# Two expert layers and an attention layer on one core: every first-layer weight split at one place, the next layer's weight conversion under a branch at one of two

## The chip, the cores and the metric

The kernel runs on one core of one Trainium2 chip. The metric is device time in microseconds (us) of one execution. The profile comes from one execution, and its times count from the start of its span.

## The reference, cut to what matters

Attention over 4 batches produces 2176 tokens of 512 values each. A router then gives each token one of 8 experts, and the expert is two matrix products with a relu between them. A third layer (two products with a convolution and a gate between) follows. In short:

```
x = attention(...)                       # 4 x 544 tokens x 512
e = argmax(x @ w_gate), or the expert of the token before where a local gate holds it
h = relu(x[token] @ w1[e])               # 512 -> 1024
out[token] = p[e] * (h @ w2[e])          # 1024 -> 512
y = (h2 * sigmoid(conv3(h2))) @ w_out,  h2 = relu(out @ w_in)
```

All of it is fp32. A product is made of three products of a high and a low part (`wh`, `wl` of a weight, `xh`, `xl` of an input), so a weight has to be split before it is used: ScalarE (ACT) casts the high part, VectorE (DVE) subtracts to get the low part.

## The kernel before

**Slots.** The tokens are sorted by expert into slots of 128. Slots 0 and 1 (`NA` is 2) are worked on beside the end of attention; slots 2 to 20 each have one `step(s)`, and slot 21 has `last`. An expert has several slots in a row. Its first slot can be a *few* slot: at most 32 tokens, for which the kernel reads the unsplit weights directly with narrow matmuls (`few()` in `layer1` and `layer2`); other slots use the split weights (`full()`).

**What one step does.** `step(s)` writes, in this order: the load of one raw chunk of the third layer's weights (`raw_load`, on SyncE's queue, SP); `layer1(s)`; the load of the next expert's first weight (`fetch(s, 1)`); the gather of slot s+3's tokens (`gather`, GpSimd, POOL); the transposes and the split of slot s+1's tokens (`turn_x(s + 1)`); the last instruction of the conversion begun one step earlier (`self.conv.pop()()`, called the pop below); the split of the first weight for slot s+1, if that slot's expert is new (`resplit(s + 1, 1)`); six DVE instructions and one POOL addition that convert the chunk of the third layer's weights from 64-bit to fp32 (`convert`, `conv64`); `layer2(s - 1)` and the load of the next second weight (`fetch(s - 1, 2)`); `turn_h(s)`, which splits the hidden values (`gh`, `gl`); and the split of the second weight if slot s's expert is new (`resplit(s, 2)`). Chunks are converted in steps 3 to 18.

**Order.** No scheduler moves anything: each engine executes its own part of this text in order, and waits on semaphores for what it reads. What an engine has in front of an instruction is therefore what the text has in front of it. Branches on a register (`tc.If`) are taken by every engine that has instructions in them, and the others pass a join.

**Two places for the first split.** The table `esi` holds in its row 1, for each slot, 0 if its expert is that of the slot before, 1 if it is new, and 2 if it is new and the slot is a few slot. A slot with 1 has its first weight split in the step before it (the early place, `resplit(s + 1, 1)`). A slot with 2 doesn't need the split weight itself; its split stands after its own `layer1` (the late place, `resplit(s, 1, late=True)`):

```
with self.tc.If(v == 2 if late else v == 1 if n == 1 else v != 0):
```

**Names in the rows.** `ws` is a raw expert weight, `wh` and `wl` its parts; `xs`, `xh`, `xl` are slot tokens; `hp` and `yp` the sums of layer 1 and layer 2; `gh`, `gl` the hidden values; `fx` a raw chunk and `wf` its conversion.

Of the kernel before, what the change touches and what calls it, by code (L numbers as in the profile page):

```python
# [13 lines left out]
ALU = mybir.AluOpType  # L14
AX = mybir.AxisListType
# [543 lines left out]
NSLOT = 25  # L559
NA = 2  # L560
NB = NSLOT - NA
# [94 lines left out]
class Routing:  # L656
# [15 lines left out]
    def tl(self, shape, name, dt=F32, tag=None):  # L672
        return self.rp.tile(shape, dt, name=name, tag=tag or name)
# [170 lines left out]
    def phase_b(self, rp, pst):  # L844
        nc, c, tl = self.nc, self.c, self.tl
        v = nc.vector
        self.rp = rp
        yield from self.front(1, pst)
        n = NT
# [46 lines left out]
        def over_s(t):  # L896
# [18 lines left out]
        esi = self.esi  # L915
        ch = tl([1, NB], "r_ch")
# [2 lines left out]
        v.tensor_reduce(nx, s1, AX.X, ALU.min)  # L919
        v.tensor_copy(esi[:, 0, NA:], es[:, 1:])  # L920
        v.tensor_copy(esi[:, 1, NA:], ch)
        v.scalar_tensor_tensor(esi[:, 1, NA + 1:NSLOT - 4], self.fw[:, 1:NB - 4], 1.0, ch[:, 1:NB - 4],
                               ALU.add, ALU.mult)
        v.tensor_copy(esi[:, 2, NA - 1:NA], es[:, 1:2])
        v.tensor_copy(esi[:, 3, NA - 1:NA], ch[:, 0:1])
        yield
# [10 lines left out]
    def few(self, b0, first):  # L937
        v, c, tl = self.nc.vector, self.c, self.tl
        sh = [1, NB, E]
        sm = tl([1, E], "r_sm")  # L940
        v.scalar_tensor_tensor(sm, b0, -128.0, first[0:1], ALU.mult, ALU.add)
        v.tensor_scalar(sm, sm, P - TS - 0.5, 1024.0, ALU.is_lt, ALU.mult)
        v.tensor_tensor(sm, sm, b0, ALU.add)
        eq = tl(sh, "r_s2")
        v.tensor_tensor(eq, sm[:, None, :].to_broadcast(sh), c.sl[0:1, :, None].to_broadcast(sh), ALU.is_equal)
        self.fw = tl([1, NB], "r_fw")
        v.tensor_reduce(self.fw, eq, AX.X, ALU.max)
        v.tensor_copy(self.esi[:, 5, NA:], self.fw)

    def late_tokens(self, s):  # L950
        v, tl = self.nc.vector, self.tl
# [72 lines left out]
class Weights:  # L1024
# [25 lines left out]
    def split(self, n, src, eng=None):  # L1050
        for k in range(len(self.t[n])):
            self.split_k(n, src, k, eng or (self.nc.gpsimd if k in POOL_K[n] else self.nc.vector))


class Moe:
# [156 lines left out]
    def last(self, s, cwr, cw):  # L1212
# [20 lines left out]
        self.fetch(s - 1, 2)  # L1233
        f2.load0()
        resplit(0, 4)
        for k in range(K_LAST, NKC - 1):
            self.l1_mm(xt, w, hp, k, range(2))
# [8 lines left out]
        for a in (0, 4):  # L1246
            self.lo_t(ht, a, t[a // 4])
        resplit(4, NFC)
        yp = self.y_tile()
        for k in range(NFC):  # L1250
# [37 lines left out]
        self.W.load(n, (self.w1, self.w2)[n - 1][bass.ds(e, 1)], **({"cond": c} if (s, n) != (0, 1) else {}))  # L1288

    def changed(self, s, pool=False):  # L1290
        return self.nc.values_load(self.rt.esi[0:1, 1, s:s + 1], min_val=0, max_val=2,
                                   engines=[mybir.EngineType.Activation, mybir.EngineType.Pool]
                                   + ([] if pool else [mybir.EngineType.DVE]))

    def resplit(self, s, n, eng=None, late=False):
        if (n == 1 and not late) or s < NA:
            self.chg[s] = self.changed(s, eng is not None)
        v = self.chg[s]
        with self.tc.If(v == 2 if late else v == 1 if n == 1 else v != 0):  # L1299
            self.W.split(n, self.W.s, eng)  # L1300

    def small(self, s):
# [4 lines left out]
    def either(self, s, few, all_):  # L1307
        with self.tc.If(self.sm[s] != 0) as c:
            few()
        with c.Else():  # L1310
            all_()

    def turn_x(self, s):
        nc = self.nc
        xs = self.xs[s]
        x = self.xt[s] = tuple(self.tp.tile([P, NKC, P], F32R, tag="x" + q, name="x" + q) for q in "hl")
        t = (self.ps if s == NA else self.px).tile([P, 4, P], F32, tag="tr", name="xlp")

        def turn():
            for k in range(NKC):  # L1320
                nc.tensor.transpose(t[:, k, :], xs[:, P * k:P * k + P], self.ident)

        def few():
            turn()
            raw()

        def raw():
            nc.scalar.copy(xs[:, 0:NKC * TS].rearrange("p (k t) -> p k t", t=TS), t[:, :, P - TS:P])

        def full():  # L1330
            turn()
            nc.scalar.copy(x[0], t)
            self.lo_t(x, 0, t)

        if s == NA:
            full()
            raw()
        else:
            self.either(s, few, full)

# [65 lines left out]
    def step(self, s):  # L1406
        W, hi = self.W, NSLOT - 3
        if NA < s <= NA + 16:
            self.raw_load(s - NA - 1)
        if s + 1 < hi - 1:  # L1410
            self.small(s + 1)
        self.layer1(s)
        if s > NA:
            self.resplit(s, 1, late=True)
        self.fetch(s, 1)
        if s + 3 < hi:
            self.xs[s + 3] = self.gather(s + 3)
        if s + 1 < hi - 1:
            self.turn_x(s + 1)
        else:  # L1420
            self.xt[s + 1] = self.hi_lo_t(self.xs.pop(s + 1), NKC, "x")
        while self.conv:
            self.conv.pop()()
        self.resplit(s + 1, 1)
        if NA < s <= NA + 16:
            self.convert(s - NA - 1)
        if s == NA:
            for _ in self.rest:
                pass
        else:  # L1430
            self.layer2(s - 1)
            self.fetch(s - 1, 2)
        self.turn_h(s)
        self.resplit(s, 2)

    def chunk(self, s):
        return (1, s // 2, 512 * (s % 2)) if s < 8 else (2, s - 8, 0)
# [422 lines left out]
```

## Time and profile before

| what | us |
|---|---|
| median of 3 runs | 645.39 (642.68 to 645.6) |
| the profiled execution, its own time | 643.43 |
| its span, first to last instruction | 641.7 |
| TensorE (PE) busy | 585.6 (91%) |
| DVE busy | 415.3 (65%) |
| ACT busy | 319.3 (50%) |
| POOL busy | 171.3 (27%) |

Attention's last products start at 149 us, slots 0 and 1 are done near 188 us, the steps run from 182 to 407 us, and the third layer's products start at 434.8 us. Which slots are new or few depends on the data; the timeline of ACT shows it, because a full slot's relu is line 1276, a few slot's is line 1352, and a weight split is line 1047 (4 casts of 1024 columns for a first weight, 8 of 512 for a second one). With the relu's start as the mark of a slot:

| slot | relu at, us | kind |
|---|---|---|
| 2 | 186.35 | few |
| 4 | 204.71 | new expert, full |
| 7 | 244.40 | new expert, full |
| 9 | 266.05 | new expert, few |
| 13 | 314.82 | new expert, few |
| 16 | 347.72 | new expert, few |
| 18 | 373.52 | new expert, full |
| 21 | 418.16 | new expert, full |

The other slots are full and go on with the expert of the slot before.

### The profile page before, as it was taken

What the parts mean: (1) busy time and instruction counts of PE and PEld (TensorE: products, weight loads), DVE (VectorE), ACT (ScalarE), POOL (GpSimd) and SP (SyncE); (2) the same over time, 40 slices, a digit from 0 to 9 for tenths busy, and PEclk for the clock granted to TensorE, in tenths of its full rate; (3) what the DMA queues carried; (4) which work ended last, traced back from release to release, by engine and by line L of the source; (5) the groups of instructions that cost most, each with busy time, mean ns of one, the idle gap of its engine ahead of it and who ended that gap; (6) DMA issues with size and microseconds to landing.
All of it is one profiled execution on the core that took longest, in us unless ns stands there. A gap on an engine that the chain in (4) does not pass through costs nothing. (4 is left out here: it accounts for less than half of the span.)

```text
span 641.7 us, 16204 instructions
## 1 busy us (share of the span) xinstructions
PE 585.6 (91%) x6066; PEld 483.6 (75%) x6066; DVE 415.3 (65%) x870; ACT 319.3 (50%) x634; POOL 171.3 (27%) x226
## 2 busy tenths in 40 slices
PE   7888888888988999979989899978899999999997
PEld 6666666766666888758767678758898998998986
DVE  7867577866956857785596984586983293393340
ACT  4754555564225454552454643665864374363331
POOL 7664910042032223223224230100032132300100
PEclk8999899999999999999999999998899999999999
DMA  8999658658047666575275673123101201000001
GB/s 223 217 218 235 186 126 189 194 194 287 18 158 272 218 210 227 185 264 197 84 261 182 247 281 125 51 89 86 50 1 51 81 3 49 34 1 34 33 35 50
DMA packets 60644, 90.57 MB, mean 141 GB/s; under 512 B 25726, under 2 KB 34198, under 8 KB 60504
## 3 DMA queue, kind: packets, MB, share of 16 engines
q1 hardware_dynamic: 57016, 78.93, 39.7%
q0 software_dynamic: 3520, 10.23, 4.7%
q8 instruction: 64, 1.05, 0.7%
q14 instruction: 44, 0.36, 0.2%
HBM read 125.87 MB, written 15.79 MB: 221 GB/s over the span
## 5 line engine op out<-in xcount | busy, mean ns | idle before, releaser
L1565 DVE SCALAR_TENSOR_TENSOR fc<-f_hp,cw,fc 128x544 f32<-128x544 f32 (+2 forms) x66 | 51.7, 784 | 72.8 <-ACT fc L1563 71.4
L1048 DVE TENSOR_TENSOR wl<-ws,wh 128x512 fp32r<-128x512 f32 (+1 forms) x92 | 74.4, 871 | 14.1 <-ACT wh L1047 12.5
L1047 ACT CAST wh<-ws 128x512 fp32r<-128x512 f32 (+1 forms) x96 | 66.2, 768 | 5.7 <-DMA ws<-in_moe_w_dram 5.3
L1128 PE MATMUL yp<-wl,gh 128*128 128x512 f32 x144 | 57.5, 399 | 3.6 <-DVEq L1299 3.3
L1128 PE MATMUL yp<-wh,gh 128*128 128x512 f32 x144 | 59.2, 411 | 1.1 <-ACTq L1299 0.9
L1128 PE MATMUL yp<-wh,gl 128*128 128x512 f32 x144 | 57.2, 397 | 0.0
L1112 PE MATMUL hp<-wl,xh 128*128 128x512 f32 x144 | 48.6, 409 | 7.7 <-DVEq L1299 7.1
L1623 PE MATMUL f<-wh,fh 128*128 128x512 f32 (+1 forms) x144 | 55.4, 385 | 0.0
L1623 PE MATMUL f<-wl,fh 128*128 128x512 f32 (+1 forms) x144 | 55.1, 383 | 0.0
L1623 PE MATMUL f<-wh,fl 128*128 128x512 f32 (+1 forms) x144 | 55.1, 382 | 0.0
L1112 PE MATMUL hp<-wh,xh 128*128 128x512 f32 x144 | 50.2, 421 | 2.8 <-ACT wh L1047 2.7
L278 ACT ACTIVATE pr<-sp,nm 128x128 f32<-128x128 f32 x128 | 36.5, 374 | 26.2 <-DVE nm L275 26.2
L1276 ACT ACTIVATE hs<-hp 128x512 f32<-128x512 f32 x36 | 19.9, 595 | 59.4 <-PE hp L1112 59.3
L1020 POOL TENSOR_TENSOR wf<-wf,fx 128x512 int32<-128x512 int32 x16 | 20.8, 1300 | 103.1 <-DVE fx L1019 75.3
L1112 PE MATMUL hp<-wh,xl 128*128 128x512 f32 x144 | 47.8, 404 | 0.0
L1073 POOL DMA_INDIRECT xs<-x_dram,gidx x22 | 26.3, 1194 | 73.6 <-ACT pr L278 34.1
L1085 POOL DMA_INDIRECT y_dram<-ys,sidx x22 | 23.6, 1070 | 70.9 <-ACT ys L1401 31.9
L1112 PEld LDWEIGHTS hp<-wl,xh 128*128 128x128 f32 x144 | 27.4, 194 | 16.8 <-DVEq L1299 9.3
L1570 ACT ACTIVATE f_hp<-f 128x544 f32<-128x544 f32 x31 | 19.4, 624 | 35.9 <-PE f L1546 35.7
L1128 PEld LDWEIGHTS yp<-wl,gh 128*128 128x128 f32 x144 | 27.2, 189 | 10.4 <-DVEq L1299 4.2
L1105 DVE TENSOR_TENSOR gl<-hlp,gh 128x512 fp32r<-128x512 f32 x36 | 23.3, 686 | 18.0 <-ACT gh L1378 16.3
L1632 ACT COPY fy<-f 128x512 f32<-128x512 f32 (+1 forms) x18 | 10.1, 563 | 48.6 <-PE f L1623 48.6
(382 smaller groups left out, 1506.3 us busy)
## 6 DMA issues: line engine op xcount, KB each, us to landing
ws<-in_moe_w_dram SPq DMA_DIRECT2D x42, 2048.0 KB
fx<-y_dram SPq DMA_DIRECT2D x17, 256.0 KB
raw<-in_k_l_dram SPq DMA_DIRECT2D x16, 256.0 KB
x_dram<-x SPq DMA_DIRECT2D x16, 256.0 KB
fx<-in_moe_w_in_dram SPq DMA_DIRECT2D x8, 512.0 KB
fx<-in_moe_w_out_dram SPq DMA_DIRECT2D x8, 512.0 KB
out_dram<-fy SPq DMA_DIRECT2D x16, 256.0 KB
VA<-in_v_l_dram SPq DMA_DIRECT2D x20, 192.0 KB
```

Of the source, the lines that this page charges most:

```text
L278: nc.scalar.activation(pr[:, hp, :], sp[:, hp, :], AF.Exp, bias=nm[:, hp:hp + 1], scale=-1.0)
L1020: nc.gpsimd.tensor_tensor(a, a, lo, ALU.add)
L1047: (cp.tensor_copy if cp else self.nc.scalar.copy)(h, src[n][:, k, :])
L1048: eng.tensor_tensor(l, src[n][:, k, :], h.bitcast(F32), ALU.subtract)
L1073: self.nc.gpsimd.indirect_dma_start(out=xs, out_offset=None, in_=self.x_dram[0:n, :], in_offset=bass.IndirectOffsetOnAxis(ap=self.rt.gidx[ ...
L1085: self.nc.gpsimd.indirect_dma_start(out=self.y_dram[:, :], out_offset=bass.IndirectOffsetOnAxis(ap=self.rt.sidx[:, s:s + 1], axis=0), in_= ...
L1105: self.nc.vector.tensor_tensor(hl[1][:, a:a + 4], t, hl[0][:, a:a + 4].bitcast(F32), ALU.subtract)
L1112: self.nc.tensor.matmul(hp[c], a[:, k, :], b[:, 512 * c:512 * c + 512], start=k == 0 and m == 0, stop=k == NKC - 1 and m == 2)
L1128: self.nc.tensor.matmul(yp, a[:, k, :], b, start=k == 0 and m == 0, stop=k == NFC - 1 and m == 2)
L1276: self.nc.scalar.activation(hs[:, 512 * c:512 * c + 512], hp[c], AF.Relu)
L1565: nc.vector.scalar_tensor_tensor(c[:, a:b], hp[:, a + t:b + t], self.cw[:, t, f:f + 1], c[:, a:b], ALU.mult, ALU.add)
L1623: self.nc.tensor.matmul(yp[:, cs], x[:, c], w[:, cs], start=f == 0 and n == 0, stop=f == NFC - 1 and n == 2)
```

## The change

Row 1 of `esi` holds only 0 or 1. The late place is gone, so a few slot's first weight is split in the step before it too. The conversion is written twice in each of steps 3 to 18, each time under a branch: at its old place if slot s+1 goes on with the same expert, and at the end of the step if slot s+1's expert is new. In the first of these steps (`turn_x` of slot 2), the copy for the few case stands ahead of the split.

```diff
@@ routing
         v.tensor_copy(esi[:, 1, NA:], ch)
-        v.scalar_tensor_tensor(esi[:, 1, NA + 1:NSLOT - 4], self.fw[:, 1:NB - 4], 1.0, ch[:, 1:NB - 4],
-                               ALU.add, ALU.mult)
...
-        self.fw = tl([1, NB], "r_fw")
-        v.tensor_reduce(self.fw, eq, AX.X, ALU.max)
-        v.tensor_copy(self.esi[:, 5, NA:], self.fw)
+        v.tensor_reduce(self.esi[:, 5, NA:], eq, AX.X, ALU.max)
@@ Moe
-    def resplit(self, s, n, eng=None, late=False):
-        if (n == 1 and not late) or s < NA:
+    def resplit(self, s, n, eng=None):
+        if n == 1 or s < NA:
             self.chg[s] = self.changed(s, eng is not None)
-        v = self.chg[s]
-        with self.tc.If(v == 2 if late else v == 1 if n == 1 else v != 0):
+        with self.tc.If(self.chg[s] != 0):
             self.W.split(n, self.W.s, eng)
...
+        def split():
+            nc.scalar.copy(x[0], t)
+            self.lo_t(x, 0, t)
+
         def full():
             turn()
-            nc.scalar.copy(x[0], t)
-            self.lo_t(x, 0, t)
+            split()
 
         if s == NA:
-            full()
+            turn()
             raw()
+            split()
@@ step
         self.layer1(s)
-        if s > NA:
-            self.resplit(s, 1, late=True)
         self.fetch(s, 1)
...
         self.resplit(s + 1, 1)
         if NA < s <= NA + 16:
-            self.convert(s - NA - 1)
+            with self.tc.If(self.chg[s + 1] == 0):
+                self.convert(s - NA - 1)
...
         self.turn_h(s)
         self.resplit(s, 2)
+        if NA < s <= NA + 16:
+            self.conv.pop()
+            with self.tc.If(self.chg[s + 1] != 0):
+                self.convert(s - NA - 1)
```

What follows are pieces of the program as each engine has it, without times. In the changed kernel the lines of the program have other numbers: 1048 becomes 1044, 1105 becomes 1101, 1014 to 1021 become 1010 to 1017, and the branches at 1299, 1303 and 1308 become 1294, 1298 and 1303.

On DVE before, between the early first split of a step (whose join is the first row) and the split of the hidden values, stand the six instructions of the conversion, whatever the next slot is:

```order
L1299 UNCONDITIONAL_BRANCH x2
L1014 TENSOR_SCALAR wf_3967<-fx 128x512
L1015 SCALAR_TENSOR_TENSOR wf_3967<-fx,wf_3967 128x512
L1016 TENSOR_SCALAR fx<-fx 128x512
L1017 TENSOR_SCALAR fx<-fx 128x512
L1018 SCALAR_TENSOR_TENSOR wf_3967<-fx,wf_3967 128x512
L1019 TENSOR_SCALAR fx<-fx 128x512
L1308 COMPARE_AND_BRANCH
L1308 UNCONDITIONAL_BRANCH x2
L1308 COMPARE_AND_BRANCH
L1308 UNCONDITIONAL_BRANCH
L1105 TENSOR_TENSOR gl<-hlp,gh 128x512 x2
```

They now stand under the branch of line 1423 there, and where it skips them the hidden split follows the weight split at once. DVE before, at the turn to the next step, after the second weight's split: the late first split stands between the step's first register load and the next slot's token split.

```order
L1303 TENSOR_LOAD esi
L1308 COMPARE_AND_BRANCH
L1308 UNCONDITIONAL_BRANCH x2
L1299 COMPARE_AND_BRANCH
L1048 TENSOR_TENSOR wl_0_2725<-ws_3446,wh_0_2724 128x1024
L1048 TENSOR_TENSOR wl_1_2727<-ws_3446,wh_1_2726 128x1024
L1048 TENSOR_TENSOR wl_2_2729<-ws_3446,wh_2_2728 128x1024
L1048 TENSOR_TENSOR wl_3_2731<-ws_3446,wh_3_2730 128x1024
L1299 UNCONDITIONAL_BRANCH x2
L1308 COMPARE_AND_BRANCH
L1308 UNCONDITIONAL_BRANCH
L1105 TENSOR_TENSOR xl<-xlp,xh 128x512
```

The same place on DVE in the changed kernel, where the first row is the branch around the second copy of the conversion:

```order
L1435 COMPARE_AND_BRANCH
L1010 TENSOR_SCALAR wf_3964<-fx 128x512
L1011 SCALAR_TENSOR_TENSOR wf_3964<-fx,wf_3964 128x512
L1012 TENSOR_SCALAR fx<-fx 128x512
L1013 TENSOR_SCALAR fx<-fx 128x512
L1014 SCALAR_TENSOR_TENSOR wf_3964<-fx,wf_3964 128x512
L1015 TENSOR_SCALAR fx<-fx 128x512
L1435 UNCONDITIONAL_BRANCH x2
L1298 TENSOR_LOAD esi
L1303 COMPARE_AND_BRANCH
L1303 UNCONDITIONAL_BRANCH x2
```

Four instructions under a branch have gone from ahead of the token split, and six under another branch have come. On POOL before, one step from its scatter to the conversion's addition reads as follows (the branch after the join of line 1308 is the late one):

```order
L1085 DMA y_dram<-ys_3453,sidx 2176x512
L1299 COMPARE_AND_BRANCH
L1299 UNCONDITIONAL_BRANCH x2
L1308 UNCONDITIONAL_BRANCH
L1299 COMPARE_AND_BRANCH
L1299 UNCONDITIONAL_BRANCH x2
L1308 UNCONDITIONAL_BRANCH
L1073 DMA xs<-x_dram,gidx 128x512
L1291 TENSOR_LOAD esi
L1299 COMPARE_AND_BRANCH
```

POOL in the changed kernel, the same piece:

```order
L1081 DMA y_dram<-ys_3453,sidx 2176x512
L1294 COMPARE_AND_BRANCH
L1294 UNCONDITIONAL_BRANCH x2
L1435 COMPARE_AND_BRANCH
L1016 TENSOR_TENSOR wf_3964<-wf_3964,fx 128x512
L1435 UNCONDITIONAL_BRANCH x2
L1303 UNCONDITIONAL_BRANCH x2
L1069 DMA xs<-x_dram,gidx 128x512
L1287 TENSOR_LOAD esi
L1294 COMPARE_AND_BRANCH
```

The second copy of the addition stands between a step's scatter and the next step's gather.

## Rows read from the trace of the kernel before

**Rows 1.** The page, busy time of an engine, share of the span, instructions.

```profile
PE 585.6 (91%) x6066; PEld 483.6 (75%) x6066; DVE 415.3 (65%) x870; ACT 319.3 (50%) x634; POOL 171.3 (27%) x226
```

**Rows 2.** Timeline of PE, steps 2 to 19: start, us, instruction [idle before, releaser].

```profile
184.25 1.93 PE L1350 MATMUL hp<-ws,xs 128*32 128x256 f32 x32 [1.75 <-ACT xs L1328]
...
199.42 0.74 PE L1112 MATMUL hp<-wl,xh 128*128 128x512 f32 x2 [0.53 <-DVE wl L1048]
...
207.29 0.50 PE L1128 MATMUL yp<-wl,gh 128*128 128x512 f32 x1 [1.78 <-DVEq L1299]
...
273.45 0.73 PE L1112 MATMUL hp<-wl,xh 128*128 128x512 f32 x2 [0.72 <-DVEq L1299]
...
286.31 0.74 PE L1112 MATMUL hp<-wl,xh 128*128 128x512 f32 x2 [3.31 <-DVEq L1299]
...
288.06 1.05 PE L1112 MATMUL hp<-wl,xh 128*128 128x512 f32 x2
...
333.31 0.73 PE L1112 MATMUL hp<-wl,xh 128*128 128x512 f32 x2 [1.63 <-DVEq L1299]
...
365.99 1.22 PE L1112 MATMUL hp<-wh,xh 128*128 128x512 f32 x2 [2.10 <-ACT wh L1047]
...
375.47 0.50 PE L1128 MATMUL yp<-wl,gh 128*128 128x512 f32 x1 [1.14 <-DVEq L1299]
```

**Rows 3.** Timeline of ACT, five places of steps 2 to 17.

```profile
182.54 0.59 ACT L1332 CAST xh<-xlp 128x512 fp32r<-128x512 f32 x1 [5.77 <-PE xlp L1321]
183.89 0.27 ACT L1328 COPY xs<-xlp 128x128 f32<-128x128 f32 x1 [0.76 <-DVE xl L1105]
...
197.06 3.89 ACT L1047 CAST wh<-ws 128x1024 fp32r<-128x1024 f32 x4 [0.98 <-DMA ws<-in_moe_w_dram]
...
307.08 0.27 ACT L1328 COPY xs<-xlp 128x128 f32<-128x128 f32 x1 [0.32 <-PE yp L1128]
...
364.90 3.89 ACT L1047 CAST wh<-ws 128x1024 fp32r<-128x1024 f32 x4 [2.48 <-DMA ws<-in_moe_w_dram]
```

**Rows 4.** Timeline of DVE, steps 3 and 4: a conversion and the two splits behind it.

```profile
202.69 0.42 DVE L1014 TENSOR_SCALAR wf<-fx 128x512 int32<-128x512 int32 x1
...
205.89 1.29 DVE L1105 TENSOR_TENSOR gl<-hlp,gh 128x512 fp32r<-128x512 f32 x2
208.40 0.69 DVE L1105 TENSOR_TENSOR xl<-xlp,xh 128x512 fp32r<-128x512 f32 x1 [1.22 <-DVEq L1299]
```

**Rows 5.** Timeline of DVE, steps 9 and 10.

```profile
275.28 0.43 DVE L1014 TENSOR_SCALAR wf<-fx 128x512 int32<-128x512 int32 x1 [1.94 <-DMA fx<-in_moe_w_in_dram]
...
278.94 5.63 DVE L1048 TENSOR_TENSOR wl<-ws,wh 128x512 fp32r<-128x512 f32 x8 [0.52 <-PE hp L1112]
284.90 0.69 DVE L1105 TENSOR_TENSOR xl<-xlp,xh 128x512 fp32r<-128x512 f32 x1 [0.34 <-DVEq L1299]
```

**Rows 6.** Timeline of SP: weight loads issued in steps 8 and 9.

```profile
258.14 5.39 SPq L1040 DMA_DIRECT2D ws<-in_moe_w_dram  x2
...
272.35 1.86 SPq L1040 DMA_DIRECT2D ws<-in_moe_w_dram  x2
```

**Rows 7.** Timeline of DVE, steps 12 and 13.

```profile
313.07 1.29 DVE L1105 TENSOR_TENSOR gl<-hlp,gh 128x512 fp32r<-128x512 f32 x2 [5.73 <-ACT gh L1378]
...
320.83 0.68 DVE L1105 TENSOR_TENSOR xl<-xlp,xh 128x512 fp32r<-128x512 f32 x1
321.43 0.68 DVE L1021 SCALAR_TENSOR_TENSOR wf<-wf,fx 128x512 int32<-128x512 int32 x1
322.26 0.43 DVE L1014 TENSOR_SCALAR wf<-fx 128x512 int32<-128x512 int32 x1
```

**Rows 8.** Timeline of DVE, step 17.

```profile
366.01 4.63 DVE L1048 TENSOR_TENSOR wl<-ws,wh 128x1024 fp32r<-128x1024 f32 x4
...
374.07 1.29 DVE L1105 TENSOR_TENSOR gl<-hlp,gh 128x512 fp32r<-128x512 f32 x2 [0.38 <-issue]
```

**Rows 9.** Timeline of POOL, the conversion's addition in step 13.

```profile
325.49 1.32 POOL L1020 TENSOR_TENSOR wf<-wf,fx 128x512 int32<-128x512 int32 x1 [9.50 <-DVEq L1308]
```

More of the change, by code (lines that the diff above doesn't have):

```diff
@@ L1290, in changed @@
     def changed(self, s, pool=False):
-        return self.nc.values_load(self.rt.esi[0:1, 1, s:s + 1], min_val=0, max_val=2,
+        return self.nc.values_load(self.rt.esi[0:1, 1, s:s + 1], min_val=0, max_val=1,
                                    engines=[mybir.EngineType.Activation, mybir.EngineType.Pool]
                                    + ([] if pool else [mybir.EngineType.DVE]))
-    def resplit(self, s, n, eng=None, late=False):
-        if (n == 1 and not late) or s < NA:
+    def resplit(self, s, n, eng=None):
+        if n == 1 or s < NA:
             self.chg[s] = self.changed(s, eng is not None)
-        v = self.chg[s]
-        with self.tc.If(v == 2 if late else v == 1 if n == 1 else v != 0):
+        with self.tc.If(self.chg[s] != 0):
             self.W.split(n, self.W.s, eng)
```

## The prediction

> **What bounds the kernel now.** I read the page first: TensorE is busy for 91% of the span [rows 1], so time can only come from the places where it waits. The timeline of TensorE alone, from 180 to 410 us, shows them. In a step between two full slots with one expert it has no gap. All gaps stand around slots 2, 4, 9, 13, 16 and 18, where an expert is new or a slot is few [rows 2]. Eight waits stand in the rows; the one at 273.45 has two more like it (for slots 14 and 17), and the one at 199.42 has one like it just before. Together that is about 15 us of waiting. After the longest wait the pairs of matmuls are slower too: a pair at 288.06 takes 1.05 us against the 0.73 of one right after a wait, which I estimate adds some 1.2 us over four such pairs; the first pair after the wait at 365.99 takes 1.22.
>
> The releasers are nearly all DVE. So I read DVE's timeline for what stood in front: a conversion that starts at 202.69 ahead of the hidden split `gl` at 205.89, which is 3.2 us, 3.1 of it the six instructions [rows 4]; the late first split and then a second split of 5.63 us behind a conversion that waits for its chunk's DMA [rows 5]. ACT's rows show two waits for a weight load [rows 3].
>
> **The change part by part.**
>
> *The conversion leaves the early place where slot s+1 is new* (steps 3, 6, 8, 12, 15, 17). In step 3, `gl` starts when the first split ends, some 3.1 us earlier; TensorE's wait of 1.78 at 207.29 [rows 2] is smaller than that, so all of it goes. In step 17, `gl` at 374.07 [rows 8] likewise comes 3.1 us earlier and the 1.14 at 375.47 goes. In step 6 nobody waits. The conversion then runs between `gl` and the next `xl`. For slot 5 that makes `xl` about 1 us later than 208.40, with TensorE still busy in layer 2 until about 211: hidden there. Terms: 1.8 and 1.1.
>
> *Slot 2's copy ahead of its split.* The copy starts at 182.54 in place of 183.89 [rows 3], so layer 1 of slot 2 starts and ends some 1.35 earlier. Slot 3's layer 1 then waits for its own `xl`, which stands behind gate work on DVE that hangs on slot 2's `xl`, now 0.3 later; I give nothing for that. But the load of slot 4's first weight is issued when layer 1 of slot 2 has read the buffer, and ACT waits 0.98 for this load at 197.06 [rows 3]. With the load 1.35 earlier that wait goes, and of TensorE's two waits, the 0.53 at 199.42 and its like, some 0.9 in all. Bounds 0 and 1.1; I take 0.9, since both waits hang on that one load.
>
> *Slots 13 and 16: the first split in the step before.* In step 12 ACT is free from the copy at 307.08 on [rows 3], so the cast starts near 307.6, and the DVE part 1.1 later (as 366.01 follows 364.90 [rows 3, 8]), to end 4.63 later at 313.3. `gl` of slot 12, at 313.07 before [rows 7], becomes 313.4 plus the price of skipping the early conversion (call it e). Then come 1.29 of `gl`, the skip of an eight-instruction second split, and the moved conversion. The skip's price is read from two rows: `xl` stands 1.22 behind `gl` where the second split was skipped [rows 4], and 0.34 behind a second split that ran [rows 5], so skipping eight instructions costs about 0.9. The conversion ends near 318.7 + e. The pop must now wait for POOL's addition (1.32 [rows 9]), so it starts near 320.1 + e, against 321.43 before [rows 7]. The chain from there (conversion, second split, next `xl`, TensorE at 333.31) is the same, with one more skip e before that `xl`. So it comes 1.3 - 2e earlier. e lies between 0.15 and 0.9: the skip of the four-instruction first split, which lies between the pop that ends at 322.11 and 322.26, takes 0.15 [rows 7]. Six instructions stand between four and eight; I take 0.3, nearer the four, because the moved block like the first split stands alone behind its branch, and book 0.7. Bounds 1.0 and -0.5. The wait of slot 14 that is like 273.45 also goes, but only moves TensorE up to the same later wait, so it isn't counted apart.
>
> For slot 16 the rows have the same form. Behind it slot 18's first weight waits for its load at 364.90 [rows 3]; that load is issued about 5 us earlier, since it no longer follows the late split, and DVE's part then follows the pop instead. DVE is nearly as late as the load was (366.01 against 364.90 [rows 3, 8]), so the gain is again the chain's 0.7, not the whole 2.10 at 365.99.
>
> *Slot 9.* Here the conversion in step 9 waits for its chunk until 275.28 [rows 5], because the chunk follows the second weight in SP's queue, and that weight is issued only when layer 2 of slot 7 has ended (the second of the two issues that begin at 258.14 and take 5.39 [rows 6]). Nothing in the change moves that. So the chain 275.28, second split at 278.94, `xl` at 284.90, TensorE at 286.31 keeps its place, the 0.72 at 273.45 only turns into a longer wait at 286.31, and one skip e is added. I book -0.3, with -0.1 and -0.9 as bounds.
>
> *The rest.* Two or three small DVE instructions fewer in the routing, and one join more per step on every engine: I put one at 0.1 us by the 0.15 of a whole skip [rows 7]. TensorE passes such joins now in every step and shows no gap between two full slots, so I book nothing; 15 of them exposed would be 1.5.
>
> **Sum.** 1.8 + 1.1 + 0.9 + 0.7 + 0.7 - 0.3 = 4.9 us. Against the profiled execution's own 643.43 (span 641.7 and 1.7 around it) that is 638.5. The median of the runs shown, 645.39, is 2 us above the profiled one; from it the sum gives 640.5. I predict **639.0**. A difference under 0.5% (3.2 us) can hardly be told from no change in this kernel.
>
> [...] The load of slot 13's first weight, issued at 272.35 before [rows 6], will now be issued near 267, while slot 9's second weight is still on its way. In the rows the chunk for step 9 landed at 275.28 with that first weight already issued 3 us before, so a later load did not visibly hold an earlier one up. [...] No run here shows a longer overlap.
>
> **The rivals.**
>
> *The branches cost what the skip of eight instructions costs.* e is 0.9. Then slots 13 and 16 lose 0.5 each in place of winning 0.7, slot 9 loses 0.9, and `gl` of slots 12 and 15 comes up to 0.9 late for TensorE. The sum is 1.8 + 1.1 + 0.9 - 1.0 - 0.9, about 2: 641.5. For it speaks the 1.22 of rows 4; against it the 0.15 for four instructions [rows 7]. [...]
>
> *The earlier first-weight load holds the second weight up* (ends slower). If from 267 on the two loads share the engines evenly, the 7 to 8 us that slot 9's second weight and chunk still need take up to 7 us more, all of it ahead of TensorE at 286.31 through the chain above. The result is 638.5 + 7 = 645.5, and some 1.5 more if the slow pairs last longer: 645 to 647. It decides from a delay of 5 us on. Against it stands the landing at 275.28.
>
> *DVE is relieved more than I count.* If e is 0.15, and slot 18 gets its weight when the load lands (near 360) because DVE reaches it in time, slots 13 and 16 give 1.0 and up to 3, and a shorter wait there spares the slow first pairs, 1 to 1.5 us: 8 to 9 us in all, 635.
>
> **How the numbers follow.** My forecast (637 to 641): 0.48. Branches at full price (641 to 643): 0.24. More relief (633 to 636.5): 0.18. Loads in each other's way (644 to 647): 0.10. The range reaches from the relief case to the upper end of the branch case, **633.5 to 643.5**, and leaves the shared loads out. Faster by over 0.5% means below 642.2: the forecast, the relief and about a third of the branch case, 0.73. Slower by over 0.5% means above 648.6, which only the far end of the load case reaches: 0.06. Same: 0.21.
>
> **What would show each step.** Right: no TensorE wait for `gl` near 205 and near 373; ACT's first split of slot 4 without a DMA wait; first splits of slots 9, 13 and 16 ahead of the copy of `ys`, in the step before; the wait at 286.31 still there, 3.5 to 5 us long; the one at 333.31 shorter by about the chain's gain. Wrong: a new wait of TensorE for `gl` of slots 8, 12 or 15; gaps of 0.5 to 1 us on DVE at the conversion's branches; the chunk of step 9 landing more than 1 us later behind its issue than before.

## The result, and the profile after

The changed kernel takes 637.64 us (median of 4 runs, 635.98 to 638.55) against 644.76 for the kernel before beside it (4 runs): a ratio of 0.990, with a 95% interval of 0.9864 to 0.9936. The profiled execution took 638.55, with a span of 636.6. The prediction was 639.0, within 633.5 to 643.5. The two medians differ by 7.1, but the two profiled spans by 5.1 (641.7 and 636.6), and larger sets of runs (e12 below, 12 and 17 of them) by 5.0; the sum of the prediction, 4.9, is to be held against these.

The page of the changed kernel, the row that answers to [rows 1]:

```profile
PE 587.8 (92%) x6066; PEld 487.0 (77%) x6066; DVE 417.0 (66%) x868; ACT 317.6 (50%) x634; POOL 174.4 (27%) x226
```

Timeline of TensorE, the waits that answer to [rows 2], and the first matmuls on a `wl` of layer 2 in steps 3 and 17, which stood behind a wait before:

```profile
190.52 0.73 PE L1108 MATMUL hp<-wl,xh 128*128 128x512 f32 x2 [1.10 <-DVEq L1294]
...
205.60 0.39 PE L1124 MATMUL yp<-wl,gh 128*128 128x512 f32 x1
...
284.96 1.09 PE L1108 MATMUL hp<-wl,xh 128*128 128x512 f32 x2 [4.73 <-DVEq L1294]
...
331.03 0.74 PE L1108 MATMUL hp<-wl,xh 128*128 128x512 f32 x2 [1.62 <-DVEq L1294]
...
364.08 1.22 PE L1108 MATMUL hp<-wl,xh 128*128 128x512 f32 x2 [2.76 <-DVE wl L1044]
...
371.34 0.39 PE L1124 MATMUL yp<-wl,gh 128*128 128x512 f32 x1
```

The waits of 1.78 and 1.14 are gone, those of 0.53 and 0.72 too. The larger ones left stand ahead of slots 3, 11, 15 and 18. At slots 11 and 18 they are longer than the 3.31 and 2.10 of before, and at slot 15 the wait is as long as it was (1.62, where it was 1.63). ACT, the answer to [rows 3]: the split of slot 4 without a wait for its load, and those of slots 9, 13 and 16 in the step before, the first of them ahead of the copy of `ys`.

```profile
197.30 3.90 ACT L1043 CAST wh<-ws 128x1024 fp32r<-128x1024 f32 x4
...
256.67 3.89 ACT L1043 CAST wh<-ws 128x1024 fp32r<-128x1024 f32 x4 [0.30 <-ACT xs L1323]
261.41 0.59 ACT L1400 COPY ys<-yp 128x512 f32<-128x512 f32 x1 [0.85 <-issue]
...
305.87 3.89 ACT L1043 CAST wh<-ws 128x1024 fp32r<-128x1024 f32 x4 [0.30 <-ACT xs L1323]
...
338.01 3.89 ACT L1043 CAST wh<-ws 128x1024 fp32r<-128x1024 f32 x4 [0.45 <-POOLq L1423]
```

DVE at slot 9, then at slots 12 to 14, the answers to [rows 5] and [rows 7]:

```profile
273.30 0.43 DVE L1010 TENSOR_SCALAR wf<-fx 128x512 int32<-128x512 int32 x1 [3.37 <-DMA fx<-in_moe_w_in_dram]
...
277.01 5.59 DVE L1044 TENSOR_TENSOR wl<-ws,wh 128x512 fp32r<-128x512 f32 x8 [0.56 <-ACT hs L1272]
283.56 0.69 DVE L1101 TENSOR_TENSOR xl<-xlp,xh 128x512 fp32r<-128x512 f32 x1 [0.95 <-DVEq L1435]
...
306.95 4.63 DVE L1044 TENSOR_TENSOR wl<-ws,wh 128x1024 fp32r<-128x1024 f32 x4 [4.28 <-ACT wh L1043]
312.10 1.29 DVE L1101 TENSOR_TENSOR gl<-hlp,gh 128x512 fp32r<-128x512 f32 x2 [0.53 <-ACT gh L1377]
313.73 0.43 DVE L1010 TENSOR_SCALAR wf<-fx 128x512 int32<-128x512 int32 x1 [0.34 <-DVEq L1294]
...
317.80 0.69 DVE L1101 TENSOR_TENSOR xl<-xlp,xh 128x512 fp32r<-128x512 f32 x1 [0.92 <-issue]
318.41 0.73 DVE L1017 SCALAR_TENSOR_TENSOR wf<-wf,fx 128x512 int32<-128x512 int32 x1
...
323.08 5.60 DVE L1044 TENSOR_TENSOR wl<-ws,wh 128x512 fp32r<-128x512 f32 x8 [0.56 <-ACT wh L1043]
329.63 0.69 DVE L1101 TENSOR_TENSOR xl<-xlp,xh 128x512 fp32r<-128x512 f32 x1 [0.95 <-ACT gh L1377]
```

Two gaps are new. `gl` starts 0.53 behind a first split, where the early conversion is skipped, and `xl` starts 0.95 behind a second split, where the late one is skipped. SP at slot 9, the answer to [rows 6]:

```profile
255.40 6.45 SPq L1036 DMA_DIRECT2D ws<-in_moe_w_dram  x2
261.95 0.52 SPq L1445 DMA_DIRECT2D fx<-in_moe_w_in_dram  x1
264.28 7.35 SPq L1036 DMA_DIRECT2D ws<-in_moe_w_dram  x2
```

With the relu's start as the mark of a slot, the two profiled executions compare as follows:

| stretch | before | after | gained | predicted |
|---|---|---|---|---|
| start to slot 1's relu | 174.65 | 176.07 | -1.42 | 0 |
| slot 1 to 4 | 30.06 | 28.88 | 1.18 | 0.9 |
| slot 4 to 7 | 39.69 | 37.63 | 2.06 | 1.8 |
| slot 7 to 9 | 21.65 | 21.68 | -0.03 | 0 |
| slot 9 to 13 | 48.77 | 49.20 | -0.43 | -0.3 |
| slot 13 to 16 | 32.90 | 31.98 | 0.92 | 0.7 |
| slot 16 to 18 | 25.80 | 25.25 | 0.55 | 0.7 |
| slot 18 to 21 | 44.64 | 43.23 | 1.41 | 1.1 |
| slot 21 to the end | 223.54 | 222.68 | 0.86 | 0 |

From slot 1 to slot 21 that is 5.66 us, where the sum said 4.9. Attention, which the change does not touch but for two small instructions, took 1.42 more.

### The profile page after: what moved, and what is told of

The parts are those of the page before. It is cut to its first block, busy times and chain, and to the rows that moved or that the text cites. A ratio compares the mean times of both kernels' runs of the same rounds, so it can differ in the third digit from the quotient of the medians.

```text
span 636.6 us, 16330 instructions
## 1 busy us (share of the span) xinstructions
PE 587.8 (92%) x6066; PEld 487.0 (77%) x6066; DVE 417.0 (66%) x868; ACT 317.6 (50%) x634; POOL 174.4 (27%) x226
## 3 DMA queue, kind: packets, MB, share of 16 engines
q8 instruction: 64, 1.05, 0.7%
## 5 line engine op out<-in xcount | busy, mean ns | idle before, releaser
L1081 POOL DMA_INDIRECT y_dram<-ys,sidx x22 | 25.7, 1170 | 99.3 <-ACT ys L1400 48.3
L1400 ACT COPY ys<-yp 128x512 f32<-128x512 f32 x15 | 8.8, 587 | 50.7 <-PE yp L1124 43.5
L1108 PEld LDWEIGHTS hp<-wh,xl 128*128 128x128 f32 x144 | 28.0, 195 | 7.0 <-DVE xl L1101 0.2
```

The costliest lines, as they stand in the source:

```text
L1081: self.nc.gpsimd.indirect_dma_start(out=self.y_dram[:, :], out_offset=bass.IndirectOffsetOnAxis(ap=self.rt.sidx[:, s:s + 1], axis=0), in_= ...
L1108: self.nc.tensor.matmul(hp[c], a[:, k, :], b[:, 512 * c:512 * c + 512], start=k == 0 and m == 0, stop=k == NKC - 1 and m == 2)
```

## The experiments

The runs of the kernel before beside these have medians of 641.6 to 642.4 us. "In the steps" is the time from slot 3's relu to slot 21's in the profiled execution; it leaves out attention, whose length differs from one execution to the next: slot 3's relu lies between 188.86 and 195.80 in the fourteen profiles. That stretch is 224.08 before and 218.12 after.

| kernel | median, us | ratio to before | in the steps | waits ahead of slots 11, 15, 18 |
|---|---|---|---|---|
| e1 | 640.4 | 0.9993 (0.9968 to 1.0017) | 226.29 | 2.84, 1.54, 2.10 |
| e2 | 642.93 | 1.0011 (0.9982 to 1.004) | 227.40 | none, 1.07, 0.61 and 0.56 |
| e3 | 638.89 | 0.9939 (0.991 to 0.9967) | 221.17 | none |
| e4 | 627.75 | 0.9782 (0.9751 to 0.9814) | 211.63 | 3.05, none, 0.83 |
| e5 | 627.45 | 0.9788 (0.9752 to 0.9825) | 211.97 | 3.35, none, 1.05 |
| e6 | 634.91 | 0.9892 (0.9861 to 0.9923) | 219.72 | 1.81, 1.79, 2.82 |
| e7 | 630.07 | 0.9833 (0.9785 to 0.988) | 213.95 | 1.79, 1.68, 2.74 |
| e8 | 623.82 | 0.9715 (0.9674 to 0.9757) | 207.09 | none, none, 0.89 |
| e9 | 633.92 | 0.9866 (0.9834 to 0.9899) | 217.20 | 4.79, 1.05, 2.16 |
| e10 | 631.89 | 0.9821 (0.978 to 0.9861) | 214.52 | 3.36, 0.51, 2.07 |
| e11 | 637.26 | 0.9918 (0.9889 to 0.9947) | 222.03 | none |
| e12 | 637.43 | 0.9918 (0.9889 to 0.9947) | 219.45 | 3.61, 1.38, 2.75 |

**Parts of the change, each alone on the kernel before.** e1 moves only the copy of slot 2:

```diff
         if s == NA:
-            full()
+            turn()
             raw()
+            split()
```

> The kernel before with one edit: for slot 2 the copy for the few case stands ahead of the token split. My theory: layer 1 of slot 2 runs 1.35 us earlier, slot 3 doesn't profit, slot 4's weight load does, and TensorE's two short waits there go: 0.9 to 1.6 us faster than the kernel before (644.8 to about 643.5). Rival: slot 3's wait takes all of it back, 644.8.

From slot 1's relu to slot 4's it took 29.26 against 30.06: 0.8 gained, near the 0.9 booked. The whole shows no difference. Its slot 4 to 5 took 16.13 against 14.59, with the same wait of 1.78: the granted clock was 0.58 from 206 to 209 us, where it was 1.00 in the stretch behind that wait before.

e2 makes only the two places of the conversion, and leaves the late split:

```diff
         if NA < s <= NA + 16:
-            self.convert(s - NA - 1)
+            with self.tc.If(self.chg[s + 1] == 0):
+                self.convert(s - NA - 1)
...
         self.resplit(s, 2)
+        if NA < s <= NA + 16:
+            self.conv.pop()
+            with self.tc.If(self.chg[s + 1] != 0):
+                self.convert(s - NA - 1)
```

> The kernel before with only the two-place conversion; the first splits of few slots stay at their late place. My theory: the waits for gl at slots 3 and 17 go (1.8 and 1.1 us and a little more), but in steps 9, 13 and 16 the moved conversion, 3.1 us, now stands ahead of the late split, so the token split behind it and TensorE come some 2.5 us later for slots 10, 14 and 17: about 3 to 5 us slower than before, 648 to 650. Rival: the moved conversion is a gain by itself wherever it stands, 641 to 642.

e3 makes only the early split (the late place and the value 2 in the table go), with the conversion unbranched at its old place:

```diff
         self.layer1(s)
-        if s > NA:
-            self.resplit(s, 1, late=True)
         self.fetch(s, 1)
```

> The kernel before with only the first splits moved to the early place; the conversion always stands at its old place, without a branch, and slot 2's copy is not moved. My theory: in steps 8, 12 and 15 the conversion now follows a 4.6 us split and makes gl of slots 8 and 12 2 to 3 us late for TensorE, which is lost again at slots 9 and 13; slot 18 gains 2.5: -2 to +1 us against before, 643 to 646. Rival: the early place alone gives most of the change, 639 to 640.

Timeline of TensorE, a row of e2 and one of e3 for the waits that each part brings alone:

```profile
317.93 0.73 PE L1112 MATMUL hp<-wl,xh 128*128 128x512 f32 x2 [3.55 <-DVEq L1299]
```

```profile
315.56 0.50 PE L1124 MATMUL yp<-wl,gh 128*128 128x512 f32 x1 [1.99 <-DVEq L1294]
```

In e2 the conversion at the end of step 12 and the late split behind it both stand ahead of the next `xl`: waits of 3.53 to 3.56 ahead of slots 10, 14 and 17. In e3 the early conversion stands between the first split and `gl`: waits of 1.97 to 2.01 for `gl` in steps 8, 12 and 15 too. Neither wait is in the changed kernel, so each part removes the wait that the other would bring. The gain of the whole does not need both, though. By its time e3 is what its rival said (639 to 640), not the theory's 643 to 646: the early split alone gives a ratio of 0.9939, against 0.9918 for the changed kernel (e12), and the two intervals overlap. The two places of the conversion alone gave nothing that can be told from zero (e2, 0.9982 to 1.004), where the theory had 648 to 650; its profiled execution is 3.3 us longer in the steps, as the theory had it.

**What the branches cost.** e4 writes the conversion at the place that the branch would choose for these slots, without a branch; the table of steps is in the program, so its time holds only for inputs with this order of slots.

```diff
+NEXT_NEW = (3, 6, 8, 12, 15, 17)
...
-        if NA < s <= NA + 16:
-            with self.tc.If(self.chg[s + 1] == 0):
-                self.convert(s - NA - 1)
+        if NA < s <= NA + 16 and s not in NEXT_NEW:
+            self.convert(s - NA - 1)
...
-        if NA < s <= NA + 16:
-            self.conv.pop()
-            with self.tc.If(self.chg[s + 1] != 0):
-                self.convert(s - NA - 1)
+        if NA < s <= NA + 16 and s in NEXT_NEW:
+            self.convert(s - NA - 1)
```

> The changed kernel with the conversion at the same place in every step as the branch chooses for this data (the end of steps 3, 6, 8, 12, 15 and 17), but written without a branch. My theory, with 0.6 us per skip on DVE as the trace of the changed kernel shows ahead of xl and about 0.45 ahead of gl: the waits at slots 11, 15 and 18 get shorter by 0.7 to 1.1 us each, 2 to 4 us faster than the changed kernel with its slow pairs, 634 to 636. Rival: the branches lie beside other work, no change, 637.6.

It is 10 us faster than the changed kernel, where the theory had 2 to 4; 6.5 of them lie in the steps: 1.6 at slot 11, 1.6 at slot 15, 3.2 at slot 18. e5 puts the branches back around the same conversions, so that each is entered and none skipped:

```diff
-            self.convert(s - NA - 1)
+            with self.tc.If(self.chg[s + 1] == 0):
+                self.convert(s - NA - 1)
```

> The kernel of the fixed places, with each conversion again under its branch, but only at the place where the branch lets it run: sixteen branches as before, none of which skips a conversion. Theory (it is the skipping of a block that costs, 0.45 to 0.95 us on DVE each): no gap of more than 0.25 us on DVE at these branches, TensorE's wait for slot 11 near 3.1 to 3.5 us, none for slot 15, and 628 to 630 us. Rival (a branch costs as much when its block is entered, or the joins on all engines cost): the waits of the changed kernel come back (about 4.7 for slot 11, 1.6 for slot 15, 2.8 for slot 18), 634 to 638 us.

The time is that of e4 (627.45 and 627.75), so a branch whose block is entered costs nothing that can be measured here. Timeline of DVE in e5, the places of the gaps of 0.53 and 0.95:

```profile
299.26 4.63 DVE L1045 TENSOR_TENSOR wl<-ws,wh 128x1024 fp32r<-128x1024 f32 x4 [4.60 <-ACT wh L1044]
304.00 1.29 DVE L1102 TENSOR_TENSOR gl<-hlp,gh 128x512 fp32r<-128x512 f32 x2
305.52 0.43 DVE L1011 TENSOR_SCALAR wf<-fx 128x512 int32<-128x512 int32 x1 [0.23 <-DVEq L1295]
...
314.72 5.65 DVE L1045 TENSOR_TENSOR wl<-ws,wh 128x512 fp32r<-128x512 f32 x8 [0.56 <-PE hp L1109]
320.29 0.68 DVE L1102 TENSOR_TENSOR xl<-xlp,xh 128x512 fp32r<-128x512 f32 x1
```

Both gaps are gone. The traces also show what fills them. `DVEq` is DVE's sequencer, which runs the branches, the register loads and the semaphore instructions of DVE's part. Lines of the views of line 1435 (276 to 284 us) and of lines 1298 and 1303 (282 to 284 us) in the changed kernel, ahead of the `xl` at 283.56; the numbers between strokes are the shortest, median and longest duration in ns, then come the first and last start in us:

```profile
L1435 DVEq COMPARE_BRANCH  x1: 63/63/63, 278.0 to 278.0; - x1
L1435 DVEq EVENT_SEMAPHORE  x1: 21/21/21, 282.6 to 282.6; - x1
...
L1298 DVEq TENSOR_LOAD <-esi x1: 316/316/316, 282.8 to 282.8; - x1
...
L1303 DVEq COMPARE_BRANCH  x2: 56/59/62, 283.1 to 283.4; - x2
```

The same register load in e5 (line 1299 there, 268 to 276 us), ahead of the `xl` that starts at 275.87:

```profile
L1299 DVEq TENSOR_LOAD <-esi x1: 316/316/316, 271.3 to 271.3; - x1
```

In the changed kernel the branch that skips was passed at 278.0, while DVE was still splitting. Behind the skipped block stands a semaphore instruction that started only when the split had ended (282.60), and the register load and the two branches of the turn to the next step ran behind it, with DVE idle. In e5, with no skip there, the load had run 4.6 us ahead of `xl`, during the split. All sixteen skips of the changed kernel have such a semaphore instruction on DVEq, ten at line 1435 and six at line 1423, and none started before the DVE instruction ahead of it had ended; the entered branches of e5 have none. Ahead of `gl` two branches stand behind it and the gap is 0.52 to 0.53, in two places three and it is 0.62. So the price of a skip here is what the sequencer has to do between it and DVE's next instruction. This is read from the traces; no run took the load or the branches out from behind a skip.

e9 and e10 add skipped copies to e5, at the late place and at the early one:

```diff
-        if NA < s <= NA + 16 and s in NEXT_NEW:
+        if NA < s <= NA + 16:
+            del self.conv[:]
             with self.tc.If(self.chg[s + 1] != 0):
                 self.convert(s - NA - 1)
```

> The kernel whose branches are all entered (627.45 us), with one thing added: in the steps whose next slot goes on with the same expert, a second copy of the conversion stands at the end of the step and is skipped there, as in the changed kernel. Theory (a skip at the end of the step costs 0.95 us on DVE and counts only where DVE's chain sets the end, behind the second splits of slots 9, 13 and 16): the wait for slot 11 goes from 3.35 to about 4.3 us, a wait of about 1 us comes for slot 15, the one for slot 18 goes from 1.05 to about 2, with some slow pairs behind them; 630 to 632.5 us. Rival (the skips on the other engines or something else than this chain make the changed kernel slower): these three waits within 0.3 us of the kernel without the skips, 627 to 629 us.

```diff
-        if NA < s <= NA + 16 and s not in NEXT_NEW:
+        if NA < s <= NA + 16:
             with self.tc.If(self.chg[s + 1] == 0):
                 self.convert(s - NA - 1)
```

> The kernel whose branches are all entered (627.45 us), with a skipped copy of the conversion at the early place in the six steps whose next slot's expert is new. Theory (an early skip costs 0.5 us on DVE and lies in the chain of slots 13 and 16 only): the wait for slot 11 stays at 3.3 to 3.4 us, one of about 0.5 us comes for slot 15 and the one for slot 18 goes to about 1.5; 628 to 629.5 us. Rival (the early skip is what costs, by making the hidden split of slots 3, 8, 12, 15 and 17 late for TensorE): waits for the hidden split of 0.5 us or more there, 630 to 633 us.

The waits came as the theory had them, to within 0.6 us. In the steps the late skips cost 5.2 us and the early ones 2.6, of which the three waits make 3.6 and 1.5. Both times lie above the theory's ranges, and e10's lies in its rival's, although the waits of that rival are not there. Most of the rest is the clock. In e9 it stands behind the longer wait for slot 18 (granted clock 0.60 and 0.84 in the two stretches of 3 us from 359 on, where e5 had 1.00 from 353 on). In e10 it stands behind a wait for slot 11 as long as e5's, 3.36 and 3.35 (0.50 and 0.63 from 283 on, against 0.79 and 0.64 from 277 on; from slot 10's relu to slot 11's 14.99 us against 14.23), so that part, some 0.8 us, can't be put down to the skips. e12 is the changed kernel again:

> The changed kernel once more, beside new runs of the kernel before, since its 637.64 us comes from other runs than the experiments. Theory (the skips account for what separates it from the kernel with entered branches: 7.0 us from slot 2's relu to the end of the span, where the late skips alone gave 5.7 and the early ones alone 2.8): 634 to 636 us here, and the same waits for slots 11, 15 and 18 (4.7, 1.6, 2.8). Rival (the kernel costs more than its skips, outside the steps): 637 us or more, with the same distance of 7.0 us inside the steps.

It came out as the rival had it, but for the wait for slot 11, which was 3.61, with another of 0.53 ahead of it. It is 7.5 us behind e5 in the steps and 10 in the median. In the two profiles the 2.6 between lie outside the steps (3.4 ahead of slot 3's relu, less 0.8 behind slot 21's), and no run tells where they come from. e6 needs no branch at all: the conversion always stands at the end of the step.

```diff
-        if NA < s <= NA + 16:
-            with self.tc.If(self.chg[s + 1] == 0):
-                self.convert(s - NA - 1)
...
-            self.conv.pop()
-            with self.tc.If(self.chg[s + 1] != 0):
-                self.convert(s - NA - 1)
+            self.convert(s - NA - 1)
```

> The changed kernel with the conversion always at the end of the step, without a branch and without knowledge of the data. Theory (skips are what costs, and the end of the step is a good place in most steps): the second weight split of slot 9 no longer stands behind the late chunk, so the wait for slot 11 falls below 3 us; in step 7 the conversion and its last instruction come ahead of slot 9's first split, which makes TensorE wait some 2 to 3 us for the hidden split of slot 8; together 626 to 631 us. Rival (a conversion behind each second-weight split delays the next token split, at slots 6, 11, 15, 18 and 20 too): waits of 1 to 3 us at several of them, 633 to 640 us.

The rival holds by its time: without a skip of a conversion the waits for slots 15 and 18 are 1.79 and 2.82, since the conversion now follows the second split and the next `xl` follows the conversion. The wait for `gl` of slot 8, 2.23, is the one expected, and the one for slot 11 did fall below 3, to 1.81.

**The chunk's load.** e7 takes the changed kernel and issues a step's chunk one step earlier, right behind the pop, ahead of the second weight's load on SP:

```diff
-        if NA < s <= NA + 16:
-            self.raw_load(s - NA - 1)
+        if s == NA + 1:
+            self.raw_load(0)
...
         while self.conv:
             self.conv.pop()()
+        if NA < s < NA + 16:
+            self.raw_load(s - NA)
```

> The changed kernel with the load of a raw chunk issued one step earlier, right behind the last instruction of the conversion whose buffer it takes, so that it no longer follows the second weight's load in SP's queue. Theory (the chunk's landing holds the chain at slot 9, as the prediction has it): conversion of step 9 without a wait for DMA, second weight's split some 3 to 4 us earlier, TensorE's wait of 4.73 for slot 11 falls below 1.5 and its slow pairs go: 632 to 635 us. Rival (the second weight's own landing holds it, or the earlier chunk puts that weight back): the wait stays above 3.5 us and the time within 1.5 us of the changed kernel's 637.6.

Timeline of DVE in e7, slot 9:

```profile
265.78 0.43 DVE L1010 TENSOR_SCALAR wf<-fx 128x512 int32<-128x512 int32 x1 [0.40 <-DVEq L1294]
...
269.49 5.60 DVE L1044 TENSOR_TENSOR wl<-ws,wh 128x512 fp32r<-128x512 f32 x8 [0.56 <-ACT wh L1043]
276.04 0.69 DVE L1101 TENSOR_TENSOR xl<-xlp,xh 128x512 fp32r<-128x512 f32 x1 [0.95 <-ACT gh L1377]
```

The wait for the DMA is gone, and the time is 2 us below the theory's range. From slot 9's relu to slot 11's it took 23.02 us against 27.52, 4.5 less; the wait ahead of slot 11 fell to 1.79, not below the 1.5 hoped for. e8 does the same on e4:

> The kernel of the fixed places (627.75 us) with the chunk's load one step earlier as well. Theory: its one long wait, 3.05 us for slot 11, falls below 1 us: 624 to 626 us. Rival: the wait stays, or turns into one for the second weight's load: 627 to 629 us.

It is the fastest, 2.9% under the kernel before, and behind slot 3 only the wait of 0.89 is left in its steps. Of the kernels here that need no knowledge of the order of slots, e7 is the fastest: 1.7% under the one before and some 7.5 us under the changed one. All of them were run on this order alone.

e11 puts the late conversion of e7 ahead of the second weight's split:

```diff
         self.turn_h(s)
-        self.resplit(s, 2)
         if NA < s <= NA + 16:
...
                 self.convert(s - NA - 1)
+        self.resplit(s, 2)
```

> The changed kernel with the chunk's load one step earlier (630.07 us) and the second place of the conversion ahead of the second weight's split in place of behind it, so that the skipped branch stands ahead of the eight instructions of that split. Theory (behind those eight the branches of the step's end are passed while DVE still works, and ahead of them the skip overlaps the wait for ACT's high part): the next token split follows the second weight's split without the gap of 0.95 us, the waits for slots 11, 15 and 18 (1.79, 1.68, 2.74) are 0.4 to 0.9 us shorter each; 627 to 629.3 us. Rival (the skip costs the same there): 629.5 to 631 us.

Both were wrong: it lost 7 us. TensorE has five waits in it, for slots 3, 8, 12, 15 and 17. Timelines of TensorE and of DVE at slot 8:

```profile
263.31 0.47 PE L1124 MATMUL yp<-wh,gh 128*128 128x512 f32 x1
266.29 0.51 PE L1124 MATMUL yp<-wl,gh 128*128 128x512 f32 x1 [2.50 <-DVEq L1294]
```

```profile
261.84 1.29 DVE L1101 TENSOR_TENSOR gl<-hlp,gh 128x512 fp32r<-128x512 f32 x2 [0.53 <-ACT gh L1377]
263.05 0.42 DVE L1010 TENSOR_SCALAR wf<-fx 128x512 int32<-128x512 int32 x1
...
265.75 0.43 DVE L1015 TENSOR_SCALAR fx<-fx 128x512 int32<-128x512 int32 x1
```

`gl` was done at 263.1, and slot 8 has no second split to run. But TensorE's next matmul reads `wl` and `gh`, not `gl`, and it was let go only when DVE had passed the branch around that split, which now stood behind the conversion that ends at 266.2. Lines of the view of the branch's line 1294 on DVEq, 261 to 267 us: its semaphore instruction, and the wait that it ended.

```profile
L1294 DVEq EVENT_SEMAPHORE  x1: 21/21/21, 266.2 to 266.2; - x1
...
  PE yp L1124: 2.5, 1
```

So the reader of the tile went on only when the branch that skips the tile's writer had been passed, 2.50 us late. The kernel before has the same at its wait of 1.78 [rows 2]. Lines of the view of line 1299 on DVEq, 207 to 208 us:

```profile
L1299 DVEq EVENT_SEMAPHORE  x1: 21/21/21, 207.2 to 207.2; - x1
...
  PE yp L1128: 1.8, 1
```

So what is called a wait for `gl` above and in the prediction is a wait for the skip of the second split, which stands right behind `gl` on DVE.

## Why the prediction came out right, and where its terms were off

**The two waits for `gl`** went as told: the terms 1.8 and 1.1 measured 2.06 and 1.41. That they are waits for the skip right behind `gl` changes nothing here, since the skip came earlier with it.

**Slot 2's copy** was booked at 0.9 and measured 0.8 alone (e1) and 1.18 in the changed kernel. In both ACT no longer waits for slot 4's load; in e1 one of TensorE's two short waits stays (0.51 at 195.77), in the changed kernel neither does.

**Slots 13 and 16** were booked at 0.7 each and measured 0.92 and 0.55, but e was mis-sized, and other errors hid it, so it is luck that their sum fits (1.47 for 1.4). I took one e of 0.3 for both places. Measured, the early skip leaves `gl` 0.53 behind the split where e5 shows no gap, and the late skip leaves `xl` 0.95 behind a second split where e5 shows none and [rows 5] show 0.34. On the other side I put a skip of 0.9 for the second split ahead of the moved conversion, and it took 0.34 (313.73). ACT's cast also began about 0.4 earlier in the step than I had it (305.87, 1.55 behind slot 12's relu). POOL's addition on the path made no difference: the turn and the `xl` that stand there took its place, and the pop followed the conversion's end by about 1.5, where I had 1.4. Together that brought the pop 1.66 earlier, counted from slot 12's relu (at 305.68 before and 304.32 after: 15.75 to 14.09, with the pop of [rows 7]), not the 1.3 - e = 1.0 of the prediction. From there to `xl` 0.74 was lost again, 0.61 of it by the late skip (0.95 for 0.34). The 0.92 is what remains. The sign that I gave for it, a shorter wait at 333.31, did not come (1.62 for 1.63), because TensorE, which no longer waits 0.71 for slot 14, came to it 0.9 earlier too, counted from slot 13's relu.

The step of the reading that failed is the one on [rows 4]: the 1.22 there is not the skip of the eight-instruction split alone. Behind it a register load, the branch of the late first split, skipped as well, and two branches of the turn lie in the same gap. Even where nothing is skipped, that turn of the step costs up to 0.92 (317.80). So e couldn't be read from the length of a block. With no load and no branch behind it the skip of four instructions takes 0.15 [rows 7], and that of eight takes 0.15 too (e4, from the end of `gl` at 258.95 to 259.10); six instructions cost 0.53 or 0.95, by what the sequencer does behind them. Gaps of 0.5 to 1 us on DVE at the conversion's branches stood in the prediction as a sign of being wrong, and they came.

**Slot 9** was booked at -0.3 and measured -0.43: the late skip took 0.61 more than the gap it replaced, and the chunk landed 0.19 sooner behind slot 9's relu. The wait at 286.31 became 4.73, within the 3.5 to 5 foretold. e7 shows that the chunk's landing held this chain, as the prediction had it.

**The rival of the branches at full price** was given 0.24, and was nearer to the truth than its number: the late skip costs the full 0.95. The early one costs 0.53, and the second split's skip 0.34 in place of 0.9, which kept its sum of 641.5 from coming true. What I did not see is its size as an opportunity: without any skip of a conversion the same change gives 627.5 for this order of slots. Blocks which are skipped cost time here (0.53 and 0.95 in the changed kernel), and blocks which are entered don't (e5). What the trace records in the gaps is a semaphore instruction, a register load and branches.

**The rival of the loads in each other's way** fell. The next first weight's load was issued from 264.28 on, 0.02 behind slot 9's relu, where the 272.35 of [rows 6] was 6.30 behind it, and the chunk landed 11.45 us behind the end of the issue ahead of it (261.85 to 273.30), against 11.75 before (263.53 [rows 6] to 275.28 [rows 5]).

**The rival of more relief** did not come: slot 18's first split still waited for DVE's chain.

**What the sum left out** is the clock. Behind two of the waits that stay, those for slots 11 and 18, TensorE's granted clock falls to about half for a while (0.52 from 285 to 288 us and 0.50 from 364 to 367 in the changed kernel). The stretches of 3 us behind the wait for slot 18, first in the changed kernel and then in e12, the same program (after the five busy columns of the engines stand the granted clock and the DMA's share and rate):

```profile
364.00:367.00 3.00, 2.92 (x7) 2.34 (x8) 3.00 (x4) 0.85 (x2) 2.02 (x1) 0.50 1.01 371
367.00:370.00 3.00, 3.00 (x15) 2.41 (x14) 2.05 (x4) 0.00 (x0) 0.00 (x0) 0.99 0.89 326
```

```profile
361.00:364.00 3.00, 2.80 (x7) 2.24 (x8) 3.00 (x4) 0.99 (x2) 2.00 (x1) 0.50 1.02 347
364.00:367.00 3.00, 3.00 (x9) 2.35 (x8) 2.05 (x4) 0.00 (x0) 0.00 (x0) 0.50 1.01 374
```

The waits are 2.76 and 2.75. Then the clock stays at its lower level (0.50) for some 3 us in the one and some 6 in the other, and slot 18 takes 13.55 us from relu to relu in the one and 14.93 in the other. This 1.4 is larger than most terms of the sum.

## What to carry to other kernels

Price a branch by what its engine's sequencer still has to do behind the skip, not by the length of its block (here 0.15 us with nothing behind the skip, 0.53 with two branches, 0.95 with a register load and two branches): find the semaphore instruction at the skip, list the loads and branches between it and the engine's next instruction, and compare with a version that has no skip there. Where a skip stands in the chain that ends last, it is worth rearranging. Put the branch around a tile's writer ahead of other long work on that engine, since here the tile's reader waited until the branch was passed even where it skipped (2.50 us in e11, 1.78 in the kernel before). When a wait goes down by a few tenths, read one relu-to-relu interval for each stretch and not the total: in this kernel attention (1.42 us between the two profiles) and the clock behind a wait (1.4 at slot 18) move the total by more.

## What the runs showed of the hardware that I had not expected

Skipping six DVE instructions cost 0.94 to 0.95 us behind a second split (five places) and 0.52 to 0.62 behind a first split (six places). An entered branch made a gap of 0.15 (e4, without it) one of 0.23 (e5) and cost nothing that shows in the total (627.75 and 627.45). At a skip DVE's sequencer ran a semaphore instruction once DVE's last instruction had ended, and what stood behind it ran with DVE idle: two branches, which began 0.2 apart (311.7 and 311.9), in the shorter gap, and a register load of 0.32 and two branches in the longer. The records of compare-and-branch instructions here last 47 to 63 ns (lines 1423 and 1435), and the gaps, which hold several instructions, 520 to 950. In two executions of the changed kernel a wait of 2.76 us was followed by a stretch of about 3 us at a granted clock of 0.50, and one of 2.75 by a stretch of about 6.
